# Transposing x by the DMA crossbar in place of TensorE for six of eight batches

## The chip, the cores and the metric

The kernel runs on one core of one Trainium2 chip. Times are device microseconds of that core.

Some names. TensorE does the matmuls, and its results stand in tiles in PSUM; ACT, DVE and POOL are the other engines, and one of them copies a result on to SBUF, where TensorE reads its operands (an evacuation). The sync queue (SP) only issues DMAs. The crossbar transpose is a DMA with `transpose=True`. PEclk is the clock that was granted to TensorE, in tenths; 5 is half clock.

## The reference

Two stages, batch by batch (8 batches, 8 heads, 512 rows of x, 32 of state, 64 wide):

```python
scores = scale * x @ state^T ;  a = softmax(scores);  xread = a @ state
scores2 = scale * state @ x^T;  a2 = softmax(scores2); sread = a2 @ x
t = concat([xread, sread], axis=2)           # 544 rows, 8 heads -> 512 columns
W = (t @ w_q) * (t @ w_k) ...                # 1/8 * einsum('bsd,btd->bst')
out = relu(einsum('bst,btd->bsd', W, t)) @ w_out
```

For `scores` TensorE needs x with its 64 columns on partitions: x transposed.

## The kernel before

All work is listed in one hand-tuned table, `ORDER`; each token is a step, a batch and an engine (t TensorE, a ACT, v DVE, p POOL). Engines run their own steps strictly in the table's order. The steps that matter:

```python
def load(n, b, e):                       # ix1..ix7: x of one batch, cast to bf16 by the DMA
    nc.gpsimd.dma_start(out=x_bf[b], in_=xsrc(b, 0, H))

def xT_mm(n, b, e):                      # two per batch, 8 transposes each
    ps = psB.tile([128, 2, NP, 128], BF, name="xT_ps", tag="psB")
    for q in range(NP):
        for u in range(2):
            nc.tensor.transpose(out=ps[:, u, q, :],
                in_=x_bf[b][:, NP * r + q, 128 * u : 128 * u + 128], identity=ident)

def xT_ev(n, b, e):                      # PSUM to SBUF, by ACT or DVE
    xT = work.tile([128, 2, NP, 128], BF, name=f"xT{r}"); copy(e, xT, ...)

def pt_mm(n, b, e):                      # the scores: waits for xT
    ... nc.tensor.matmul(lhsT=L[b][f"xTe{r}"][:, u, q, :], rhs=stT[...])

def fs_ev(n, b, e):                      # state rows of four batches, one store
    nc.sync.dma_start(out=out[4 * j : 4 * j + 4, S:SP, :], in_=ost)
# ... (cut)
```

The softmax here doesn't subtract the row's maximum and nothing guards it: scores larger than these inputs give would overflow.

## Time and profile before

| | before |
|---|---|
| time, median of 2 | 95.85 us (95.74 to 95.96) |
| span | 93.4 us |
| TensorE busy | 79.8 us, 85% |
| xT on TensorE | 128 transposes, 16 groups of 0.45 us at full clock |
| DMA engines | full from about 12 to 33 us, the loads of x |
| after the last matmul | 5.6 us |

TensorE sets the time: from 29.2 to 88 us it is idle for 0.36 us. The prediction below shows the lines and how they are read.

### The profile page before, as it was taken

The page shows a single profiled execution, that of the slowest core. Times are in us where ns is not written, and L with a number is a line of the kernel's source. Part 1 is how long each engine was busy: PE and PEld are TensorE (multiplying, and loading weights), DVE is VectorE, ACT ScalarE, POOL GpSimd, SP SyncE. Part 2 cuts the span into 40 slices and gives each one's busy share as a digit, 9 for nine tenths or more (in the row PEclk, how much of TensorE's full clock was granted, in tenths as well). Part 3 has the DMA queues.
Part 4 walks back from the last instruction along what each step waited for, and adds up shares of the span by engine and source line. Part 5 has one row for each costly group of instructions (what it writes and reads, how often), then busy time and mean ns, then how long its engine had stood idle before and what let it go on. Part 6 is the DMA issues. An engine that isn't in the chain of part 4 may idle for free.

```text
span 93.4 us, 3134 instructions
## 1 busy us (share of the span) xinstructions
PE 79.8 (85%) x1376; PEld 53.4 (57%) x1376; DVE 56.2 (60%) x109; ACT 53.6 (57%) x80; POOL 44.6 (48%) x58
## 2 busy tenths in 40 slices
PE   5908098998995999999999999999999999999500
PEld 3506086896864676888366547646668644444100
DVE  1026948589584959896496198965786487222500
ACT  2324746687894687359967647864054876444200
POOL 7307994894499989899500009339750000000000
PEclk9998555599999999999999999999999999999985
DMA  1998799999999915500032517806455004428990
GB/s 28 305 260 193 94 160 156 205 203 194 197 199 197 201 18 232 225 11 0 0 130 102 225 22 213 311 30 270 186 225 232 0 0 164 173 39 300 400 363 21
DMA packets 12933, 15.13 MB, mean 162 GB/s; under 512 B 1592, under 2 KB 10296, under 8 KB 12856
## 3 DMA queue, kind: packets, MB, share of 16 engines
q0 software_dynamic: 7808, 4.19, 33.2%
q1 hardware_dynamic: 4280, 9.70, 29.3%
q10 hardware_dynamic: 832, 1.05, 3.8%
q8 instruction: 10, 0.16, 0.7%
q14 instruction: 3, 0.02, 0.1%
HBM read 10.22 MB, written 8.91 MB: 205 GB/s over the span
## 4 chain that ended last, share of the span: by engine, by line
PE 76%; ACT 6%; DMA 6%; DVE 4%; issue 2%; DVEq 0%
PE fin_ps L538 30%; PE xT_ps L246 9%; DMA st_f<-in_state_dram 6%; PE pt_ps L264 5%; PE mix_ps L504 5%; PE at_ps L322 4%; PE srd_ps L335 3%; PE wq_ps L398 3%; PE wk_ps L436 3%; DVE stT L139 3%; ACT xT L137 2%; PE fins_ps L538 2%; PE srd_ps L348 2%; PE v_ps L468 2%; PE g_ps L452 2%
## 5 line engine op out<-in xcount | busy, mean ns | idle before, releaser
L538 PE MATMUL fin_ps<-w_o,rmix 128*128 128x512 bf16 x128 | 30.0, 379 | 0.0
L309 POOL TENSOR_TENSOR A<-E,rinv 128x1024 bf16<-128x1024 bf16 (+1 forms) x9 | 15.3, 1718 | 15.5 <-DVE rinv L303 15.5
L538 PEld LDWEIGHTS <-rmix 128*128 128x128 bf16 x128 | 11.6, 98 | 12.5 <-ACT rmix L143 0.3
L137 ACT COPY ost<-fin_ps 128x1024 f32<-128x1024 f32 (+1 forms) x10 | 9.3, 928 | 14.1 <-PE fin_ps L538 13.6
L139 DVE COPY ost<-fin_ps 128x1024 f32<-128x1024 f32 (+1 forms) x8 | 8.7, 1089 | 11.1 <-PE fin_ps L538 7.5
L280 ACT ACTIVATE E<-pt_ps 128x512 bf16<-128x512 f32 x16 | 9.6, 603 | 4.3 <-PE pt_ps L264 4.3
L372 POOL TENSOR_TENSOR sbd<-srn,mask 128x256 bf16<-128x256 bf16 x16 | 9.5, 612 | 4.4 <-DVE srn L362 4.1
L295 DVE TENSOR_REDUCE rsum<-E 128x16 f32<-128x512 bf16 x16 | 10.6, 672 | 1.1 <-ACT E L280 1.1
L246 PE MATMUL xT_ps<-ident,x_bf 128*128 128x128 bf16 x128 | 11.0, 238 | 0.1
L145 DVE TENSOR_SCALAR rmix<-mix_ps 128x1024 bf16<-128x1024 f32 x7 | 8.5, 1223 | 2.7 <-PE mix_ps L504 2.6
L137 ACT COPY xT<-xT_ps 128x1024 bf16<-128x1024 bf16 x9 | 9.1, 1020 | 1.5 <-PE xT_ps L246 1.5
L143 ACT ACTIVATE rmix<-mix_ps 128x1024 bf16<-128x1024 f32 x9 | 9.3, 1032 | 0.7 <-PE mix_ps L504 0.5
L213 POOL TENSOR_TENSOR stbd<-st_bf,mask 128x256 bf16<-128x256 bf16 x16 | 9.3, 614 | 0.0
L246 PEld LDWEIGHTS <-x_bf 128*128 128x128 bf16 x128 | 8.4, 106 | 1.0 <-issue 0.4
L264 PE MATMUL pt_ps<-stT,xT 128*128 128x64 bf16 x128 | 7.1, 203 | 0.5 <-DVE xT L139 0.4
L504 PE MATMUL mix_ps<-wq,V 64*128 64x256 bf16 x64 | 5.7, 272 | 1.2 <-issue 1.1
L152 POOL DMA_DIRECT2D x_bf<-in_x_dram x7 | 6.6, 944 | 0.0
L264 PEld LDWEIGHTS <-xT 128*128 128x128 bf16 x128 | 5.6, 105 | 1.6 <-DVE xT L139 0.5
L139 DVE COPY xT<-xT_ps 128x1024 bf16<-128x1024 bf16 x7 | 4.8, 686 | 2.2 <-PE xT_ps L246 2.0
L139 DVE COPY AT<-at_ps 128x1024 bf16<-128x1024 bf16 x7 | 4.8, 685 | 1.2 <-PE at_ps L322 1.2
L322 PE MATMUL at_ps<-ident,A 128*128 128x128 bf16 x64 | 5.0, 219 | 0.0
L504 PEld LDWEIGHTS <-V 64*128 64x128 bf16 x64 | 2.4, 94 | 3.8 <-issue 2.8
(76 smaller groups left out, 115.9 us busy)
## 6 DMA issues: line engine op xcount, KB each, us to landing
out_dram<-ost SPq DMA_DIRECT2D x14, 512.0 KB, 3.8
x_bf<-in_x_dram POOLq DMA_DIRECT2D x7, 512.0 KB, 13.4
out_dram<-ost SPq DMA_DIRECT2D x4, 256.0 KB, 2.1
st_f<-in_state_dram SPq DMA_DIRECT2D x1, 512.0 KB, 5.6
x_f<-in_x_dram ACTq DMA_DIRECT2D x2, 256.0 KB, 4.3
x_f<-in_x_dram SPq DMA_DIRECT2D x2, 256.0 KB, 6.3
w_o<-in_moe_w_out_dram POOLq DMA_DIRECT2D x1, 512.0 KB, 10.5
out_dram<-ost ACTq DMA_DIRECT2D x2, 256.0 KB, 3.9
```

Source lines behind the costliest of these rows:

```text
L137: nc.scalar.copy(out=out, in_=in_)
L139: nc.vector.tensor_copy(out=out, in_=in_)
L143: nc.scalar.activation(out=out, in_=in_, func=AF.Relu)
L213: nc.gpsimd.tensor_tensor(out=stbd[:, b, r], in0=st_bf[:, b, r : r + 1, :].to_broadcast((128, NP, D)), in1=mask[:, :, None].to_broadcast(( ...
L246: nc.tensor.transpose(out=ps[:, u, q, :], in_=x_bf[b][:, NP * r + q, 128 * u : 128 * u + 128], identity=ident,)
L264: nc.tensor.matmul(out=ps[:, 2 * u : 2 * u + 2, NS * q : NS * q + NS], lhsT=L[b][f"xTe{r}"][:, u, q, :], rhs=stT[:, b, :, NP * r + q, :], ...
L280: nc.scalar.activation(out=L[b]["E"][:, r].rearrange("p c q n -> p c (q n)"), in_=L[b][f"pt{r}"], func=AF.Exp, scale=float(scale),)
L295: nc.vector.reduce_sum(out=L[b]["rsum"][:, w], in_=L[b]["E"].rearrange("p r c q n -> p (r c q) n")[:, w], axis=AX.X,)
L309: eng.tensor_tensor(out=L[b]["A"].rearrange("p r c q n -> p (r c q) n")[:, w], in0=L[b]["E"].rearrange("p r c q n -> p (r c q) n")[:, w], ...
L372: nc.gpsimd.tensor_tensor(out=L[b]["sbd"][:, r], in0=L[b]["srn"][:, r : r + 1, :].to_broadcast((128, NP, D)), in1=mask[:, :, None].to_broa ...
L504: nc.tensor.matmul(out=ps[:, h, kk, :], lhsT=L[b]["V"][rows, 128 * k : 128 * k + 128], rhs=L[b]["wq"][rows, 0:SH], start=True, stop=True,)
L538: nc.tensor.matmul(out=ps, lhsT=lhs(k), rhs=w_o[:, k, :], start=(k == 0), stop=(k == KC - 1))
```

## The change

Its intent: take 96 of the 128 transposes off TensorE, and 12 of 16 evacuations off ACT and DVE, by letting the DMA engines' crossbar transpose x from SBUF to SBUF; and reorder the table to suit.

```diff
+    def x_dT(n, b, e):
+        xT = work.tile([128, H, 2, 128], BF, name="xTd")
+        nc.sync.dma_start(
+            out=xT.rearrange("p h u t -> p (h u) t"),
+            in_=x_bf[b].rearrange("p h f -> p (h f)"),
+            transpose=True,
+        )
+        for r in range(2):
+            L[b][f"xTe{r}"] = xT[:, NP * r : NP * r + NP].rearrange("p q u t -> p u q t")
-        xT = work.tile([128, 2, NP, 128], BF, name=f"xT{r}")
+        xT = work.tile([128, 2, NP, 128], BF, name=f"xT{r}", bufs=2)
-    tail = ctx.enter_context(tc.tile_pool(name="tail", bufs=6))
+    tail = ctx.enter_context(tc.tile_pool(name="tail", bufs=5))
 ORDER (cut; the tokens around the crossbar steps, "s" is the sync queue):
+... pt0.1.t xs.2.s sums.0.t ... sums.1.t stbd.1.p at1.0.t ... pt0.2.t ...
+... oe0.0.a wq.2.t rinv.3.v xs.5.s ... g.2.t xs.4.s ... pt0.5.t ... pt0.4.t ...
+... wq.3.t ix6.0.p ... ix7.0.p ... xs.6.s fs.3.t wqe.4.a fin1.2.t fse.3.v xs.7.s ... pt0.6.t
+... fin1.5.t fs.7.t oe0.5.v fse.7.a           (end of the table)
```

A second new function, the same for the attention weights A, is defined and not used in the table.

## The prediction

> **What bounds the kernel now.** I read the page first, then the stretches, then the chain of waits in order of time, then the DMA issues. The page:
>
> ```profile
> PE 79.8 (85%) x1376; PEld 53.4 (57%) x1376; DVE 56.2 (60%) x109; ACT 53.6 (57%) x80; POOL 44.6 (48%) x58
> PE   5908098998995999999999999999999999999500
> ...
> PEclk9998555599999999999999999999999999999985
> DMA  1998799999999915500032517806455004428990
> ...
> L246 PE MATMUL xT_ps<-ident,x_bf 128*128 128x128 bf16 x128 | 11.0, 238 | 0.1
> ...
> L137 ACT COPY xT<-xT_ps 128x1024 bf16<-128x1024 bf16 x9 | 9.1, 1020 | 1.5 <-PE xT_ps L246 1.5
> ...
> L139 DVE COPY xT<-xT_ps 128x1024 bf16<-128x1024 bf16 x7 | 4.8, 686 | 2.2 <-PE xT_ps L246 2.0
> ```
>
> The second line is TensorE in 40 slices of 2.33 us: nearly every slice from the sixth on is full. PEclk is half in slices 5 to 8. The DMA row shows the engines full from slice 6 to slice 14, and mostly free later. The stretches say the same in numbers; their columns are the stretch, its length, the busy time of PE, PEld, DVE, ACT and POOL, then the clock, the DMA share (over 1 where records overlap) and GB/s:
>
> ```profile
> 9.30:18.70 9.40, 6.85 (x149) 5.75 (x150) 6.45 (x12) 6.13 (x8) 7.88 (x10) 0.50 1.14 153
> 18.70:29.20 10.50, 8.92 (x248) 7.27 (x245) 7.52 (x18) 9.07 (x15) 7.89 (x12) 0.99 1.44 198
> 29.20:60.00 30.80, 30.80 (x548) 21.19 (x549) 23.30 (x41) 20.86 (x32) 18.62 (x23) 1.00 0.47 132
> 60.00:88.00 28.00, 27.64 (x350) 15.36 (x348) 16.29 (x29) 13.93 (x22) 6.11 (x6) 1.00 0.43 163
> ```
>
> From 29.2 to 88 us TensorE is idle for 0.36 us; no other engine is near it. Before that it waits a little. The chain of waits (start, length, what) gives these pieces:
>
> ```profile
> 24.21 0.46 PE xT_ps L246 x8
> ...
> 24.69 1.94 ACT xT L137 x2
> ...
> 28.07 1.08 issue
> ...
> 42.46 0.45 PE xT_ps L246 x8
> ...
> 87.77 0.59 ACT ost L137
> ```
>
> Eight transposes (half of one batch) cost 0.45 us of TensorE at full clock. The named waits are 1.94 us for two evacuations of transposed x, 1.08 us, and 0.32 us at 22.6. TensorE ends at 87.77; the last copy and store make 5.6 us of tail to 93.4. The measured time is 2.45 us above the span. So this is a TensorE-bound kernel after 29 us, and in the early part one bound by the arrival of x and the half clock. When x arrives comes from the DMA issues:
>
> ```profile
> x_bf<-in_x_dram POOLq DMA_DIRECT2D x7, 512.0 KB, 13.4
> ```
>
> Narrowing that view to single issues gives issue plus time to landing: batch 1 at 8.2+7.2=15.4, batch 2 at 9.1+8.8=17.9, batch 3 at 10.9+12.4=23.3, batch 4 at 12.5+13.4=25.9, batch 5 at 28.8, batch 6 at 31.2, batch 7 at 33.9. The loads land in order, one each 2.6 us, w_o being between batches 2 and 3.
>
> **What the Trainium skill says.** "VectorE: DVE Perf Modes", section The three transpose paths, lists a 128x128 bf16 transpose at 390 ns on TensorE and 1309 ns by the DMA crossbar. The trace disagrees on TensorE: 238 ns a piece, 56 ns apart. No run here shows the crossbar yet. "Advanced Engine Details and Errata", section DMA Advanced Topics, expects 350 to 400 GB/s from crossbar transposes; "DMA: Bandwidth & Descriptors", section Latency and other measured facts, gives 261 GB/s for one that was measured. Nothing here shows either. "TensorE: Matmul & The Clock Gate", section Part 1, says that the clock is judged over free-running windows of about 3.4 us and halves after an idle one; the trace agrees in kind: two idle pieces of 2.4 us (4.65 to 7.08 and 9.1 to 11.5) are followed by half clock in slices 5 to 8.
>
> **The change part by part.**
>
> Removed from TensorE: 12 groups of eight transposes, 12 x 0.45 = 5.4 us. Removed from ACT and DVE: 12 of 16 evacuations; two stay on each engine, so ACT loses 7 x 1.02 = 7.1 us and DVE 5 x 0.69 = 3.4 us. Neither is a bound after 29 us, so this pays only through the 1.94 us wait and through PSUM buffers.
>
> Added: six crossbar transposes of 128x2048 bf16, 512 KB each, all on the sync queue, which also carries the stores. Length of one, an estimate: if it moves rows of 128 elements (256 B), that is 2048 pieces, 128 on each of 16 engines. The trace's packet records show 1024 packets of 256 B (the w_q and w_k loads) at a median of 18 ns, so 128 x 18 = 2.3 us of service (228 GB/s, a little under the skill's 261). The fixed part, from the skill's 1309 ns less eight such pieces per engine (0.14 us), is about 1.2 us. So 3.5 us alone. While loads fill the engines I double the service: 5.8 us. I call this length T.
>
> Moved: the loads of batches 6 and 7 are issued later from POOL; the matrix cast goes from POOL to DVE; two batches' final products (batch 0's second half, much of batch 4) are moved to the end as filler. The tail keeps its form (copy of 0.6 us, one 256 KB store), so I keep 5.6 us. One tail buffer fewer binds nothing that I see.
>
> To place the transposes I gave every TensorE step the time that its group takes in the chain at full clock (final product 0.86, scores 0.23, v 0.56, wq 0.45, mix 0.33, transposes of A 0.45, and so on) and added along both tables: 70.7 us before, 65.3 after. The old one ends at 87.77, so 17.1 us lie outside its sum: 13.3 by 18.7 us (late start and half clock), 3.3 in the three named waits, 0.5 elsewhere. If the new one kept only the 13.3, it would end at 78.6, a time of 86.7 us: the floor, never reached if the transposes are late. Position plus lag gives when TensorE asks, to set against when the data is there:
> - Batch 2: asked at 7.0+13.3 = 20.3. There at 17.9+5.8 = 23.7. Wait 3.4, lag 16.7.
> - Batch 3: its load lands 2.3 later than before, behind the first transpose's traffic: 25.6+5.8 = 31.4. Asked at 12.1+16.7 = 28.8. Wait 2.6, lag 19.3.
> - Batch 5, queued behind the first store, which follows a final product ending at 14.7+19.3 = 34.0 plus 1.1 for its copy; the engines are free now, so 35.1+3.5 = 38.6. Asked at 18.7+19.3 = 38.0. Wait 0.6, lag 19.9.
> - Batch 4, next in the queue, 2.3 later: 40.9 against 20.5+19.9 = 40.4. Wait 0.5, lag 20.4.
> - Batch 6: loaded from about 21+20.4 = 41.4, landed by 47; its transpose also queues behind a store at 47.0, done 50.5. Asked at 31.4+20.4 = 51.8. No wait. Batch 7: 54.0 against 54.9. No wait.
>
> Sum: 65.3+20.4 = 85.7, tail 5.6, offset 2.45: 93.7 us. I add 0.8 us for waits that stay as in the old kernel once copies are gone: 94.5 us. In other words, of 5.4 us of saved work and 3.3 us of old waits, 7.1 us come back as waits for the crossbar.
>
> **The rivals.**
> 1. Fast crossbar: T is 3.5 everywhere, since the loads yield to it. Then the waits are 1.1, 1.9, 0.6 and 0.5, 4.1 in all, and the time is 93.7-3.0+0.8 = 91.5 us. For it: the table was made by someone who placed the steps only about 3 us of TensorE work ahead of their use (2.7 us for batch 6), so a length near 3 us was in mind. Against: the DMA row is full to slice 14.
> 2. Slow crossbar: the queue issues the pieces slowly or the loads win each turn, T is 8 or more. Batches 2 and 3 then wait 5.6 and about 3.5, and stalls of that length can cost a window of half clock, some 2 us of work each: 99 us or more. For it: the two idle pieces before the half clock in the trace were only 2.4 us long. Against: later transposes meet nearly free engines.
> 3. Only TensorE counts: the queue is always ahead, and the gain is just the 5.4 us: 90.4 us. Against: batch 2's x lands at 17.9 and is asked for at 20.3, which leaves 2.4 us, less than my 3.5 for one alone.
> 4. Another engine takes over: ACT and DVE lose work and POOL keeps its sum (44.6 us), so I give this little.
>
> **Range and chances.** Each us on T moves batches 2 and 3 by roughly 1.0 to 1.3 us in the end, so T between 3.5 and 8 gives 91.5 to 99. Below it lies the case where even old waits vanish, 89.5; above it lost clock windows, 101. Range 89.5 to 101. Faster by over 2% means below 93.9, which my sum nearly meets and the fast case does: 0.46. Within 2% (93.9 to 97.8): 0.26. Slower: 0.28.
>
> **What would show it.** Right: TensorE waits for DMA xTd at the first scores of batches 2 and 3, of 2 to 4 us each; under 1 us at batches 4 to 7; landing of the crossbar DMAs near 5 to 6 us early and 3.5 later; TensorE busy about 5.4 us less; PEclk without new 5s after slice 8. Wrong: median landing above 8 us, or below 3; half-clock slices after 20 us; waits at batches 6 and 7, which would mean that late loads or stores ahead in the sync queue hold the transposes; a load landing much later than 2.3 us behind its old place.

## The result

The changed kernel took 119.91 us (119.48 to 120.33), before 95.85. A ratio here is the mean time of one kernel's fast runs over that of the other's of the same rounds, so not quite the ratio of the medians: 1.251, interval 1.231 to 1.271. That is outside my range of 89.5 to 101.

The page of the changed kernel, lines that answer to those of before:

```profile
span 117.7 us, 2944 instructions
PE 80.0 (68%) x1270; PEld 51.0 (43%) x1280; DVE 51.1 (43%) x97; ACT 50.3 (43%) x81; POOL 44.1 (37%) x57
...
PE   6565898000099999059999591099999999999000
...
PEclk9975559555555999756999999859999999999975
DMA  4996999999940008999909959904026043857720
...
DMA xTd<-x_bf 30%; PE fin_ps L555 21%; DMA x_bf<-in_x_dram 7%; PE pt_ps L281 4%; PE mix_ps L521 3%; PE at_ps L339 2%; PE wk_ps L453 2%; PE g_ps L469 2%; PE wq_ps L415 2%; PE srd_ps L352 2%; PE v_ps L485 2%; POOL stT L165 1%; ACT ost L135 1%; PE v_ps L494 1%; PE wk_ps L441 1%
...
L281 PE MATMUL pt_ps<-stT,xTd 128*128 128x64 bf16 x96 | 5.7, 224 | 22.6 <-DMA xTd<-x_bf 22.6
```

TensorE is as busy as before in microseconds (80.0 against 79.8) though 96 transposes are gone (the records show 1270 matmuls for 1376; ten of the final product's are missing from them). Part of it ran at half clock: from 30 to 40 us, TensorE was busy for 7.8 us at a granted clock of 0.59. PEclk has 5s in the middle, where before had none after slice 8. The TensorE row has holes of several slices. The chain of work that ended last is crossbar for 30% of the span, and the scores' row says what they waited for: 22.6 us, all for `xTd`.

TensorE in order of time, only the scores of the crossbar batches (start, busy time, what, and in brackets the wait before and for what):

```profile
32.24 1.03 PE L281 MATMUL pt_ps<-stT,xTd 128*128 128x64 bf16 x16 [11.73 <-DMA xTd<-x_bf]
39.96 0.63 PE L281 MATMUL pt_ps<-stT,xTd 128*128 128x64 bf16 x16
51.15 0.61 PE L281 MATMUL pt_ps<-stT,xTd 128*128 128x64 bf16 x8 [4.15 <-DMA xTd<-x_bf]
...
54.55 0.98 PE L281 MATMUL pt_ps<-stT,xTd 128*128 128x64 bf16 x16
67.70 0.64 PE L281 MATMUL pt_ps<-stT,xTd 128*128 128x64 bf16 x16 [1.30 <-DMA xTd<-x_bf]
...
76.33 0.61 PE L281 MATMUL pt_ps<-stT,xTd 128*128 128x64 bf16 x8 [5.39 <-DMA xTd<-x_bf]
```

Batch 2 waits 11.7 us, batch 3 not, batch 5 4.15, batch 4 not, batch 6 1.3, batch 7 5.4. The same in the chain, where the first line is batch 2's load, the next pieces are transposes from issue to landing (the third spans those of batches 6 and 7), and the last line is the last copy:

```profile
8.99 8.55 DMA x_bf<-in_x_dram
17.56 14.64 DMA xTd<-x_bf
...
44.36 6.74 DMA xTd<-x_bf
...
62.24 14.04 DMA xTd<-x_bf x2
...
109.02 0.58 ACT ost L135
```

The first transpose took 14.6 us. Most of the reason is in the DMA view of the stretch 22 to 30 us, when it runs beside the loads (queue, packets, MB, share), and by the same view of 32.2 to 33.2 us, when the loads are done and the second transpose runs alone:

```profile
q0 software_dynamic: 1921, 0.97, 87.8%
q1 hardware_dynamic: 1944, 0.50, 46.6%
```

```profile
DMA packets 1127, 0.29 MB, mean 289 GB/s; under 512 B 1127, under 2 KB 1127, under 8 KB 1127
...
q1 hardware_dynamic: 1127, 0.29, 128.0%
```

Beside the loads the crossbar's queue moved 1944 rows in 8 us, the load's queue 1921: one for one. That is 243 rows a us, or 62 GB/s at 256 B a row, and 8.4 us for a batch's 2048 rows. Alone it moved 1127 rows in 1 us, 289 GB/s. Ahead of the rows lie 4.2 us: the queue took 5.5 us to issue this transpose, and there are next to no rows before 21.8 us. That makes 12.6 of the 14.6 us. The last 2 us are not explained: by 30.2 us as many rows had moved as one batch has (the second transpose, issued from 23.8 us on, may have some of them), and from 30.5 to 32.1 us, with the loads nearly over (54 pieces), only 569 rows moved.

Also, the last matmul ends at 109.0 and the span at 117.7: a tail of 8.7 us, not 5.6.

### The profile page after: what moved, and what is told of

It reads as the page before. It is cut to its first block, busy times and chain, and to the rows that moved or that the text cites. A ratio compares the mean times of both kernels' runs of the same rounds, so it can differ in the third digit from the quotient of the medians.

```text
span 117.7 us, 2944 instructions
## 1 busy us (share of the span) xinstructions
PE 80.0 (68%) x1270; PEld 51.0 (43%) x1280; DVE 51.1 (43%) x97; ACT 50.3 (43%) x81; POOL 44.1 (37%) x57
## 4 chain that ended last, share of the span: by engine, by line
PE 46%; DMA 37%; issue 5%; POOL 3%; ACT 1%; SPq 0%; POOLq 0%
DMA xTd<-x_bf 30%; PE fin_ps L555 21%; DMA x_bf<-in_x_dram 7%; PE pt_ps L281 4%; PE mix_ps L521 3%; PE at_ps L339 2%; PE wk_ps L453 2%; PE g_ps L469 2%; PE wq_ps L415 2%; PE srd_ps L352 2%; PE v_ps L485 2%; POOL stT L165 1%; ACT ost L135 1%; PE v_ps L494 1%; PE wk_ps L441 1%
## 5 line engine op out<-in xcount | busy, mean ns | idle before, releaser
L555 PE MATMUL fin_ps<-w_o,rmix 128*128 128x512 bf16 x118 | 30.8, 394 | 0.8 <-issue 0.4
L281 PE MATMUL pt_ps<-stT,xTd 128*128 128x64 bf16 x96 | 5.7, 224 | 22.6 <-DMA xTd<-x_bf 22.6
L555 PEld LDWEIGHTS <-rmix 128*128 128x128 bf16 x128 | 11.7, 100 | 12.7 <-issue 1.7
L281 PEld LDWEIGHTS <-xTd 128*128 128x128 bf16 x96 | 4.8, 119 | 24.5 <-DMA xTd<-x_bf 23.5
L137 DVE COPY ost<-fin_ps 128x1024 f32<-128x1024 f32 (+1 forms) x9 | 9.9, 1105 | 8.9 <-PE fin_ps L555 8.9
L135 ACT COPY ost<-fin_ps 128x1024 f32<-128x1024 f32 (+1 forms) x9 | 8.3, 918 | 5.2 <-PE fin_ps L555 4.5
L244 PE MATMUL xT_ps<-ident,x_bf 128*128 128x128 bf16 x32 | 4.1, 311 | 1.4 <-DVE x_bf L137 0.5
L143 DVE TENSOR_SCALAR rmix_s<-mixs_ps 128x128 bf16<-128x128 f32 x6 | 1.6, 288 | 7.2 <-PE mixs_ps L541 7.2
L135 ACT COPY srT<-srT_ps 128x256 bf16<-128x256 bf16 x7 | 2.6, 374 | 4.6 <-PE srT_ps L398 4.6
L339 PEld LDWEIGHTS <-A 128*128 128x128 bf16 x64 | 4.2, 104 | 0.7 <-issue 0.2
L507 ACT ACTIVATE V<-v_ps 128x512 bf16<-128x512 f32 x6 | 3.6, 597 | 1.2 <-PE v_ps L494 1.1
```

The lines of the kernel that those rows point to most:

```text
L135: nc.scalar.copy(out=out, in_=in_)
L137: nc.vector.tensor_copy(out=out, in_=in_)
L143: nc.vector.tensor_scalar(out=out, in0=in_, scalar1=0.0, scalar2=None, op0=ALU.max)
L281: nc.tensor.matmul(out=ps[:, 2 * u : 2 * u + 2, NS * q : NS * q + NS], lhsT=L[b][f"xTe{r}"][:, u, q, :], rhs=stT[:, b, :, NP * r + q, :], ...
L339: nc.tensor.transpose(out=L[b]["at"][:, r, c, :], in_=L[b]["A"][:, r, c, :, :], identity=ident)
L555: nc.tensor.matmul(out=ps, lhsT=lhs(k), rhs=w_o[:, k, :], start=(k == 0), stop=(k == KC - 1))
```

## The experiments

My theory after reading the trace: the 24 us are waits for the crossbar, longest where its rows take turns with a load, and half clock behind them. The rival: the reordered table costs time of its own. Runs 1 to 4, 5 to 8 and 9 to 11 shared a chip each, with their own runs of the kernel before (medians 95.75, 95.24 and 95.55 us). The changed kernel was measured beside a median of 95.85, so a difference in us from it, or from one group of runs to another, is good to about 0.6 us; the ratios are free of that.

A rival for small differences is the early half clock of the kernel before (slices 5 to 8), since the profile of the seventh experiment has none. But over the 24 fast runs of before here the mean clock goes from 0.907 to 0.995, and the 13 runs at 0.95 or more were no faster (median 95.61 us) than the 11 below (95.24); the run of the seventh experiment at 0.935 took 93.57 us, no longer than its others.

### 1. The new table, transposes back on TensorE

```diff
-xs.2.s ... xs.7.s
+xT0.2.t xTe0.2.v xT1.2.t xTe1.2.a        (and so for 3 to 7, three TensorE steps ahead of use)
```

> The new table with all six crossbar transposes put back on TensorE, each pair three TensorE steps before its first use. Main theory (the waits for the crossbar and the half clock they bring cost the time, the new order does not): no DMA wait on TensorE, time 93 to 98 us. Rival (the new order itself, with its late loads of batches 6 and 7 and its moved final products, costs much of the 24 us): 104 us or more.

Measured: 102.39 us (101.79 to 103.40), ratio 1.069 (1.059 to 1.079). This lies between my two figures and is neither theory's. The table with transposes put back by hand is 6.6 us slower than before, with no wait for a crossbar. The profile is of the slowest run, called slow, but it has the same structure. Half of the 6.6 lies at the end:

```profile
91.19 0.88 PE fins_ps L557 x4
92.08 0.58 ACT ost L137
```

The last matmul ends at 92.1, the span at 100.7: a tail of 8.6 us, 3.0 more than before. The last step is now the store of the state rows. Other waits stand where I wedged the transposes in, for their evacuations (up to 0.8 us each). So the crossbar accounts for some 17.5 us over this kernel, and the table is not free.

### 2. The old table with the crossbar

```diff
-xT1.2.t ... xT0.2.t xTe1.2.a ... xTe0.2.v        (and so for 3 to 7)
+xs.2.s
```

> The old table, with the crossbar in place of TensorE's transposes for batches 2 to 7. Main theory (crossbar rows take turns with the load's rows while loads run): the first transpose again needs 12 to 16 us from issue to landing, TensorE waits over 10 us for it, and the total is at least as bad as the changed kernel, 115 to 128 us. Rival (the new order is at fault): under 106 us.

Measured: 110.69 us (110.66 to 110.73), ratio 1.158. The waits of TensorE (total, times, longest):

```profile
PE pt_ps L282 <- DMA xTd<-x_bf: 16.0, 3, 11.1
```

The mechanism is as expected (an 11.1 us wait at batch 2; batch 3's transpose is a piece of 16.8 us in the chain), the total below my 115: the old table asks late for batches 6 and 7 and loads them early, so only 16.0 us of waits arise. The crossbar costs 14.9 us over before in the old table too (which got the smaller buffers as well). The new order is not its cause.

### 3. Batches 2 and 3 back on TensorE

```diff
-xs.2.s ... xs.3.s
+xT0.2.t xTe0.2.v xT1.2.t xTe1.2.a ...           (and so for 3)
```

> The changed kernel with only batches 2 and 3 put back on TensorE. Main theory: the 11.7 us wait and the half-clock stretch after it go, and what stays are waits of some 4 us for batch 5 and some 5 us for batch 7: 100 to 106 us. If the crossbar only hurts while loads run, the time is under 100; if all six cost alike (4 us each), about 111.

Measured: 110.12 us (109.85 to 110.38), ratio 1.152. This is more than the main theory's 100 to 106. It is nearest to the third figure, about 111 for six transposes that cost alike, but the waits are not alike: 3.9 us at batch 5, 0.4 at 4, 2.5 at 6 and 2.9 at 7. In all they fell from 22.6 to 9.7 us, but the time by only 9.8, since four groups of transposes (1.8 us) are back on TensorE, with waits of their own. So the late transposes hurt as well, with no load of x in the way of the last of them. Something else had to stand in front.

### 4. A store moved behind the last transpose

```diff
-... fin1.2.t fse.3.v xs.7.s ...
+... fin1.2.t xs.7.s fse.3.v ...
```

> The changed kernel with the store of the state rows of batches 0 to 3 (256 KB, split four ways) issued behind the transpose of batch 7 and not ahead of it. Theory A (rows of the transpose stand behind that store's rows in the same rings): the wait of 5.4 us for batch 7 falls below 2 us, and the time to 115 to 117 us. Theory B (the queue's issue of a transpose, 3.1 to 5.7 us, sets it whatever is ahead): the wait stays above 4 us, 119 to 121 us.

Measured: 112.76 us (both runs), ratio 1.180: 7.2 us better than the changed kernel (6.8 by the ratios) by swapping two tokens. In the changed kernel the DMA row of 66 to 72.7 us, in 40 slices, and the GB/s show less than 100 GB/s for 2.7 us from 67.2 us on, where the store stands. TensorE still has work until 70.9 us, then it waits for this transpose:

```profile
DMA  9999996128300332100231667999922225222792
GB/s 219 219 217 217 220 202 131 38 49 49 12 0 0 12 12 12 12 0 37 49 61 53 96 107 150 257 271 194 160 98 98 110 89 130 66 67 46 128 255 46
```

With the swap the chain has one piece of 5.6 us there in place of 14.0 for two, and TensorE no longer waits at batch 7:

```profile
62.25 5.57 DMA xTd<-x_bf
```

So the store ahead of it made this wait, as theory A has it, and the time is below its 115 to 117 us. From the scores of batch 6 to those of batch 7 it took 5.6 us less; another 1.3 us came behind them, where the changed kernel ran at half clock (0.50 from 76.3 to 79 us) and this one at full. That the rows stood behind the store's in the same rings is not shown. Why the store's pieces were so slow between two transposes, about 1 us each in the records, no view shows.

### 5. The loads of 3, 4, 5 and w_o issued later

```diff
-... ix2.0.p iwo.0.p ... ix3.0.p ... ix4.0.p ... ix5.0.p ... stbd.1.p ...
+... ix2.0.p ... stbd.1.p ix3.0.p iwo.0.p ix4.0.p ix5.0.p ...
```

> The changed kernel with the loads of batches 3, 4 and 5 and of w_o issued behind POOL's early work (from about 20 us), so that the engines are idle while batch 2 is transposed. Theory (its rows took turns with the load's rows): the first transpose falls from 14.6 us, issue to landing, to 5 to 7 us and TensorE's wait at batch 2 from 11.7 to 3 to 5 us; batch 3's then meets the later loads and waits more. Rival (a transpose this early is slow on its own, for instance because the queue issues it slowly): still over 11 us. Total 112 to 120 us.

Measured: 121.93 us (120.97 and 122.89); one run, the profiled one, counts as slow, so I take only the order of events from it. TensorE at batches 2 and 3:

```profile
23.23 0.64 PE L282 MATMUL pt_ps<-stT,xTd 128*128 128x64 bf16 x16 [1.28 <-DMA xTd<-x_bf]
...
39.26 1.03 PE L282 MATMUL pt_ps<-stT,xTd 128*128 128x64 bf16 x16 [8.77 <-DMA xTd<-x_bf]
```

The first transpose was issued at 17.65 and its scores started at 23.23: 5.6 us, with no load running, against 14.6; the queue's issue of it took 3.5 us against 5.5. TensorE's wait fell from 11.7 to 1.3 us. Batch 3's transpose now ran beside the later loads, 11.1 us in the chain, and waited 8.8. The wait went where the loads went. The rival (slow on its own) is out: the loads stretch both the issue and the rows.

### 6. TensorE kept busy in the wait

```diff
+    def filler(n, b, e):
+        for _ in range(b):
+            nc.tensor.matmul(out=ps, lhsT=zero[:, 0:128], rhs=zero, start=True, stop=True)
-... swe.2.a pt0.2.t ...
+... swe.2.a fil.95.t pt0.2.t ...
```

> The changed kernel with 95 matmuls on zeros (about 10 us at full clock) on TensorE ahead of the first scores of batch 2, that is in the wait. Theory (the stall brings the half clock, and that costs on top): full clock from 21 to 38 us of the profile, 2 to 4 us less in total, 116 to 118 us. Rival (half clock there is hidden by other waits): 119 to 121 us.

Measured: 115.95 us (115.91 to 115.99), ratio 1.217: 4.0 us less than the changed kernel (3.2 by the ratios), for useless work. The clock row, to set against the changed kernel's above:

```profile
PEclk9995556999999999976999967859999999999855
```

Slices 8 to 17 are full now. From the first scores of batch 2 to those of batch 3 it took 5.8 us in place of 7.7, a gain of 1.9 us. This part is the clock's. The remainder came behind: the store ahead of batch 5's transpose was ready sooner (the wait for it was 2.6 in place of 4.15 us), and the wait at batch 7 was 2.3 in place of 5.4 us. Why that one fell, no run isolates.

### 7. The old table, batches 5, 6 and 7 only

```diff
-xT1.5.t ... xTe1.5.v ... xT0.5.t ...             (and so for 6 and 7)
+xs.5.s xs.6.s xs.7.s                             (where xT1.5.t stood, ahead of the first store)
-        xT = work.tile([128, H, 2, 128], BF, name="xTd")
+        xT = work.tile([128, H, 2, 128], BF, name="xTd", bufs=3)
```

> The kernel before with batches 5, 6 and 7 alone on the crossbar, all three issued ahead of the first store and used late. Theory (a crossbar transpose is harmless where it has ended before TensorE asks): no DMA wait on TensorE, six groups of 0.45 us less, 2.7 us off: 92.5 to 94 us. Rival (the transpose still holds up loads, stores or TensorE's clock): 95.5 us or more.

Measured: 93.60 us (93.57 to 93.85, 4 runs) against 95.24 of before in the same rounds: ratio 0.9835, interval 0.9797 to 0.9873. The time is in the range that I had written, and it beats both kernels. (As in the changed kernel, the buffers of xT on TensorE went from 4 to 2.) The sync queue:

```profile
29.24 11.01 SPq L260 DMA_TRANSPOSE xTd<-x_bf  x3
```

Three transposes occupy it from 29.2 to 40.3 us; the first took 7.5 us to land, the third 5.6; TensorE asks first at 41.3 and never waits for them. Of the 2.7 us of saved work 1.6 arrive. The lead over the kernel before, read at the same steps of both timelines, is 0.3 us at the last scores before a group leaves (29.71 and 29.44), 0.7 at the v step of batch 1 (39.29 and 38.58), 1.0 at that of batch 4 (55.84 and 54.85) and 1.45 at the wq step of batch 7 (68.67 and 67.22). The first 0.3 us are thus not the crossbar's, and the six groups return 1.15 us, about 0.2 of their 0.45 us each: the first 0.4, the next three together 0.3, the last two 0.45. The chain shows one place after the first:

```profile
40.69 0.34 PE mix_ps L522 x4
...
41.06 0.76 ACT rmix L142
...
41.98 0.59 ACT E L298
42.57 0.93 ACT rmix L142
...
43.54 1.89 PE fin_ps L556 x8
```

The final product at 43.54 is held by the relu of mix on ACT (the 0.76 and 0.93), with an exponential between; TensorE waits 0.23 us for it. In the old table a group of transposes stood in such places. That they filled a gap there is my reading; no run isolates it.

### 8. The store of state rows split in four

```diff
-        nc.sync.dma_start(out=out[4 * j : 4 * j + 4, S:SP, :], in_=ost)
+        for i in range(4):
+            nc.sync.dma_start(out=out[4 * j + i, S:SP, :], in_=ost[32 * i : 32 * i + 32])
```

> The changed kernel with each store of state rows (4 x 32 x 512) issued as four stores of 32 x 512. Theory (the one store of four parts runs on few of the engines and the rows of batch 7's transpose stand behind it there): the wait at batch 7 falls from 5.4 us below 3, the tail after the last matmul from 8.7 to about 6.5 us, in total 112 to 116 us. Rival (any store ahead of the transpose holds it, however it is split): wait unchanged, 118 us or more.

Measured: 111.65 us (111.49 to 111.81), ratio 1.172: 8.3 us less than the changed kernel (7.5 by the ratios), and a little under the 112 to 116 that I expected. The wait at batch 7 fell from 5.4 to 2.2 us, its transpose from 9.5 to 5.1 us, and the queue's issue of that from 5.7 to 3.0:

```profile
67.75 5.11 DMA xTd<-x_bf
...
104.28 0.02 issue
104.30 0.58 ACT ost L136
```

And the tail, 104.3 to 109.9, is 5.6 us again. So the one store of shape 4 x 32 x 512 is slow in itself: at the end of the table it costs 3.1 us, and between two transposes it holds the second. That fits a store that runs on few of the engines, and so does the DMA view: from 114 to 116 us of the changed kernel this store alone takes 23.2% of the time of the 16 engines, the worth of 3.7; from 107 to 109 us of this run the four stores take 40.5%.

### 9. A free crossbar

```diff
     def x_dT(n, b, e):
-        (the crossbar transpose)
-            L[b][f"xTe{r}"] = xT[...]
+            L[b][f"xTe{r}"] = L[1][f"xTe{r}"]     # wrong data on purpose
```

> Wrong results on purpose: the changed kernel with the crossbar transposes left out, batches 2 to 7 taking their scores from batch 1's transposed x. It shows what the new table is worth if the crossbar were free. My tally of the prediction, with the 3 us longer tail that the changed kernel showed: 86.7+3.1 = 89.8 us, so 89 to 93. If the table has waits of its own beside the crossbar's, 96 us or more.

Measured: 93.93 us (93.50 to 94.36), ratio 0.983. It lies between my two figures, a miss. The new table without any crossbar is only 1.6 us better than the kernel before in the same rounds (95.55); so the crossbar costs 119.9 - 93.9 = 26.0 us in it (25.7 by the ratios). Its scores are wrong: the check does not see a wrong x here, so "correct" for the other runs does not speak for the transposes.

### 10. Batch 4 on the crossbar as well

```diff
-xT1.4.t ... xTe1.4.v ... xT0.4.t ... xTe0.4.a
+xs.4.s xs.5.s xs.6.s xs.7.s                      (where xT1.4.t stood)
```

> The seventh experiment with batch 4 on the crossbar too. In the old table TensorE asks for batch 4 at 29 to 30 us, and its x lands near 26 while three loads still run. Theory (a transpose costs only where it ends after TensorE asks, and its rows take turns with the load's): one wait of 7 to 11 us at batch 4, with a stretch of half clock behind it, 101 to 107 us. If batch 4 is as cheap as 5 to 7: 92.5 to 94 us.

Measured: 103.63 us (103.56 to 103.70), ratio 1.084. This is one more batch than in the seventh experiment, and 10.0 us more (9.6 by the ratios). The buffers differ too: four for xTd, five in the tail. The only wait for the crossbar:

```profile
PE pt_ps L282 <- DMA xTd<-x_bf: 8.8, 1, 8.8
```

As expected in wait and time. The piece in the chain is 26.51 to 37.99, 11.5 us from issue to landing, beside the loads of 5, 6 and 7 for most of it.

### 11. The transposes of A of batches 4 and 7

```diff
-at.4.t ... ate.4.v ... at.7.t ... ate.7.v
+as.4.s ... as.7.s                                (behind A.4.p and A.7.p; otherwise as in the seventh)
```

> The seventh experiment with the transposes of A of batches 4 and 7 on the crossbar as well (256 KB each; A of batch 7 is ready 10 us ahead of its use, that of batch 4 about 4.5). If both end in time: 0.9 us less of TensorE, 92.5 to 93.2 us. If batch 4's stands behind the two stores ahead of it in the queue: a wait of 1 to 3 us at its first use, 94 to 96 us.

Measured: 95.34 us (94.99 to 95.99, 6 runs), ratio 0.998. The time lies in the second branch, but that branch's wait is not there: no wait for a crossbar, and no gain. It is 1.7 us slower than the seventh experiment (1.4 by the ratios), with 0.9 us less work on TensorE. In the profiled runs 1.2 us of it are there by the first scores of batch 1 (17.82 and 19.00), up to where the two kernels have the same work; batch 1's load landed at 15.9 there, at 14.9 in the seventh. Later two relus on DVE, of 1.2 us each, stand in the chain before a final product, which waits 0.6 us for the second:

```profile
56.50 0.34 PE mix_ps L522 x4
...
56.86 1.22 DVE rmix L144
...
58.55 1.22 DVE rmix L144
...
59.81 0.38 PE fin_ps L556
```

What moved the early microsecond I did not find out, and one profile does not say that all six runs have it: the profiled run is the second slowest of them, 0.5 us above their median.

## Why the prediction was wrong, point by point

- **What bounds the kernel, and what is removed: right.** The new table without a crossbar is a TensorE-bound kernel again, and six groups of transposes off the old table gained 1.6 us.
- **The step that failed: "While loads fill the engines I double the service: 5.8 us. I call this length T."** T was 14.6 us at batch 2. Two things were missing. Beside the loads the records have one crossbar row of 256 B for each load piece of 512 B (1944 to 1921), so rows went at 62 GB/s and not at half of 228; and 4.2 us of the queue's issue stand ahead of the rows. Some 2 us more stay open. The fifth experiment shows that the loads are the cause, by moving them: 5.6 us. Rival 2 ("the queue issues the pieces slowly or the loads win each turn, T is 8 or more", with half clock behind) was what happened, though the turns were equal; I worked it out with a T of 8 and closed my range at 101. Its signs came too, as I had listed them: half clock after 20 us, and waits at batches 6 and 7.
- **Batch 3, "Wait 2.6": none came.** The 11.7 us at batch 2 had given its transpose the time. Its load landed 0.5 us later than before, not 2.3.
- **"So 3.5 us alone": mis-sized.** With no load running it was 4.6 to 7.0 us from issue to landing where no store of state rows was near, of which the issue alone is 1.5 to 4.2, in half of the cases 3.0 to 3.2. That, and not my schedule, made the 4.15 us at batch 5: issue to asking was 2.9 us in my table and 2.6 in the trace.
- **"Batch 7: 54.0 against 54.9. No wait": wrong.** The wait was 5.4 us. I placed its transpose behind a store in the queue and let the store pass for nothing; that store stopped it (experiments 4 and 8).
- **"The tail keeps its form": wrong by 3.1 us.** I looked at the size of the last store, 256 KB as before, and not at its shape, 4 x 32 x 512.
- **Half clock: named as rival 2's penalty, left out of the sum.** At the first wait it cost 1.9 us directly, and 3.2 to 4.0 with what came behind (experiment 6). The early half clock, which the sum did contain, goes with no longer time in the runs of before.
- **The floor of 86.7 us: too low.** With a free crossbar the time was 93.9: some 2.8 of the 7.2 us are the tail (8.4 in that run); the rest are waits that the tally of TensorE's steps cannot see.

The 26.0 us that the crossbar costs in the new table are thus 22.6 us of direct waits and about 3.4 of the rest, half clock for the most part by my reading. What stays open: the last 2 us of the first transpose, why the store's pieces crawl between two transposes, and the early microsecond of the eleventh experiment.

## What to carry to other kernels

In these runs a DMA that took work off a busy engine was worth only what it finished before that engine asked. So put its measured length, with the traffic of that moment, against the time from data ready to first use, transfer by transfer. Here that leaves batches 5 to 7 and 1.6%, and one batch more costs 10 us. And look at what stands ahead of it in the same queue, by shape as well as by size.

## What the Trainium skill lacked or had wrong

- "Advanced Engine Details and Errata", section DMA Advanced Topics, expects 350 to 400 GB/s of a crossbar transpose. Alone, rows went at 289 GB/s at best; 512 KB in 5.6 us, issue to landing, is 94 GB/s; beside loads the rows went at 62 GB/s. What it costs beside other traffic is not on the page.
- "DMA: Bandwidth & Descriptors", section Queues, rings and completion order, says that an engine goes round its queues by packets. The runs agree in kind: the counts of the two queues were equal (1944 rows to 1921 load pieces in 8 us); how many rows go in one turn they do not show. The page does not draw the consequence for a queue of 256 B rows.
- I found no page with the time for which a transpose of this size holds the issuing queue of this chip: 3.0 to 3.2 us for 512 KB in half of the cases with no load running (1.5 to 4.2 in all), 1.4 to 1.6 us for 256 KB, 5.5 and 7.7 us beside loads. ("DMA: Bandwidth & Descriptors" has cycle counts for "previous generations", without naming this chip.)
- "DMA: Bandwidth & Descriptors", section Why a DMA increments its semaphore by 16 and not by 1, says that a transfer issued from the sync queue uses the largest number of engines, up to 16, that divides the outermost dimension of both its sides, so four where one side is 4 x 32 x 512. The runs agree: the store took the time of 3.7 engines, and splitting it took 3.1 us off the tail. The 2.7 us at less than 100 GB/s while a transpose stands behind such a store are on no page.
